# A fused top-k attention and MLP kernel: the second weights converted later, two conversion operations and a check moved in GpSimd's queue, and 16 more units turned by VectorE

## The chip, the cores and the metric

The kernel runs on one core of a Trainium2 chip. The metric is the device time of one execution in microseconds, the median of several runs. One further execution was profiled, and all views below are of it. The engines are named TensorE (PE in the profile, PEld for its weight loads), VectorE (DVE), ScalarE (ACT), GpSimd (POOL) and SyncE (SP, which only issues DMAs here).

## The reference, cut to what matters

```python
scores = scale * np.matmul(q, k.transpose(0, 1, 3, 2))      # q, k, v: (8, 8, 576, 64), float32
kth = np.partition(scores, -32, axis=-1)[..., -32:-31]
scores = np.where(scores >= kth, scores, -1e9)
attn = np.exp(scores - scores.max(-1, keepdims=True))
attn = attn / (attn.sum(-1, keepdims=True) + 1e-9)
x = np.matmul(attn, v)                                       # bridged to (8, 576, 512)
xn = (x - x.mean(-1, keepdims=True)) / np.sqrt(x.var(-1, keepdims=True) + 1e-6) * g_ln
out = x + np.maximum(xn @ w_ch1, 0) @ w_ch2                  # 512 -> 2048 -> 512
```

The MLP's two weights arrive as 64-bit floats and are turned into float32 on the chip.

## The kernel before

**Units and steps.** The attention is cut into 160 units. A unit is 128 query rows of two heads (two tiles of 128 x 576 scores), or, for the last 64 rows of a sequence ("rest"), the 64 rows of both heads in one tile. Four units of one kind, one for each pair of heads, or longer groups such as rows [0-1, rest] and [2-3], follow each other batch by batch. The main loop runs over steps n; in step n several units stand at different stages, and each engine executes its instructions in the order in which the loop writes them.

- `scores` (L395, copied by L376) is done two steps ahead: TensorE makes the score halves, ScalarE copies them from PSUM to `sc`.
- `halve` (L416, L417) at the end of step n makes the larger and the smaller half of the next unit's scores. `select` in four parts (L438, L424, L430) then finds the 32nd largest score by maxima of eight and replacements. All of this is on VectorE. The pool of `hi` has two buffers.
- `prepare` (L450, L451) scales the threshold and the maximum on ScalarE, `mask` is a Relu on ScalarE (L486) and a subtraction on GpSimd (L489), and `weigh` is the exponential with its row sum (L497). The pool of `e` has two buffers.
- A unit's weights must then be turned for the product with v. Either TensorE does it (`turn`: L555 for the main part, copied by L567; L584 for the ends, copied by L585), or the unit is "moved": VectorE transposes 32 x 32 blocks (`move`, L528), SP sends them to DRAM and three steps later `bring` fetches them in turned order, and TensorE turns the ends only. Units from the 40th on are moved, but for rest units and the last unit of a group: 72.
- `values` (L609, L616) is the product with v for a group; `take_values` (L624) copies it, `place` turns it back (L651) and scales it into the rows x (L628). A group's `lag` is the number of steps from its last unit to `values`: 2 for units 0-7, then 3, or 4 where the next job's first unit is moved.

**The note.** `watch` (L457, GpSimd) notes for each unit whether the eighth maximum of the smaller half could have mattered. Every 16 units `settle_watch` (L466) reduces the notes; at the end `tell` decides whether a slower second pass runs (it doesn't for these inputs). Before, step n begins with the note of unit n-1:

```python
        if mk and doubt is not None:
            watch(mk)
```

**Weights.** 32 pieces of 128 x 512, 16 of w1, then 16 of w2. `fetch` is a DMA of 512 KB; `split` runs three activations (L163 size, L164 low word, L167 sign), for w1 a fourth that multiplies the sign by the norm's gain (L169), then a clamp on GpSimd (L170); `shift` is on VectorE (L173); `join` is an integer addition and a multiplication on GpSimd (L179, L181). The list `batches` says which pieces are split in which step: four ahead of the loop, one or two in steps 0-7, two in each of steps 8-15. A batch's pieces are joined one step later. Up to step 6 the joins stand at a step's end.

**MLP blocks.** When a block of 256 finished rows is there, its matmuls go into the list `todo`, and `fill` puts some of them between the attention's instructions, as many as `slot` plans from estimated costs. The first block is given at step 9 (`gives_first`); its path values, take_values, place, statistics (L679), turning (L713), hidden matmuls (L754) is straight-line there, and its rows of w2 are needed for its second product (L793). After it GpSimd forms sums of w2's quarters (`form_pair`, L965-L968, four operations a pair, four pairs), which later blocks use in a product with seven instead of eight parts (L911, with sums L841-L847 on GpSimd). After the last unit only MLP work is left.

Of the kernel before, what the change touches and what calls it, by code (L numbers as in the profile page):

```python
# [10 lines left out]
ALU = mybir.AluOpType  # L11
# [8 lines left out]
STEEP = 2.0**90  # L20
# [9 lines left out]
def compute(  # L30
# [12 lines left out]
    nc = tc.nc  # L43
    P = nc.NUM_PARTITIONS
# [46 lines left out]
    def const(shape, name):  # L91
        return consts.tile(shape, FP32, tag=name, name=name)
# [5 lines left out]
    def turned():  # L98
        return brief("tp")
# [5 lines left out]
    ends = const([P, P], "ends")  # L105
    nc.gpsimd.memset(ends[:], 0.0)
    if doubt is not None:
        watched = const([P, 34], "watched")
        nc.gpsimd.memset(watched[:], -1.0)
    ident = const([P, P], "ident")  # L110
    make_identity(nc, ident[:])
# [10 lines left out]
    class Piece:  # L122
# [26 lines left out]
        def split(self):  # L149
            i = self.i  # L150
            high = self.raw[:, :, 1].bitcast(FP32)
            if i < NF:
                self.size = hpool.tile([P, DM], U32, tag="h", name="size")[:]
                self.low = wt_rows[:, i % 8]
                homes = ((opool, "o"), (opool, "o"), (rpool, "r"), (rpool, "r"), (xtpool, "xT"))
            else:
                self.size = wt_rows[:, 2 * i % 8].bitcast(U32)
                self.low = wt_rows[:, (2 * i + 1) % 8]
                homes = ((opool, "o"), (opool, "o"), (rpool, "r"))
            pl, tag = homes[i % len(homes)]  # L160
            self.sign = pl.tile([P, DM], FP32, tag=tag, name="sign")
            size_f = self.size.bitcast(FP32)
            nc.scalar.activation(size_f, high, AF.Abs)  # L163
            nc.scalar.activation(  # L164
                self.low, self.raw[:, :, 0], AF.Copy, bias=2.0, scale=2.0**-51
            )
            nc.scalar.activation(self.sign[:], high, AF.Sign)  # L167
            if self.i < NF:
                nc.scalar.mul(self.sign[:], self.sign[:], gcol[:, self.c : self.c + 1])  # L169
            nc.gpsimd.tensor_scalar(size_f, size_f, HIGH_MAX, HIGH_MIN, ALU.min, ALU.max)  # L170

        def shift(self):
            nc.vector.tensor_scalar(  # L173
# [22 lines left out]

    batches = {}
    queue = list(pieces)
    for n in range(-1, NF):
        count = 4 if n < 0 else 1 + (n + 1) % 2 if n < NF // 2 else 2  # L200
        batches[n], queue = queue[:count], queue[count:]
    assert not queue

# [2 lines left out]
    def weights(n, phase):  # L206

        now, before = batches.get(n, []), batches.get(n - 1, [])  # L210
        if phase == 0:
            for x in batches.get(n + 1, []):
                x.fetch()
            for x in now[0::2]:
                x.split()
        elif phase == 1:
            for x in before:
                x.join()
            for x in now[1::2]:
                x.split()  # L220
# [149 lines left out]
    def scores(u):  # L370

        u.sc = scpool.tile([P, 2, S], FP32, tag="sc", name="sc")
        made = [score_half(u, s) for s in range(2)]
        for t in range(len(u.tiles)):
            for s in range(2):
                nc.scalar.copy(  # L376
                    u.sc[:, t, s * HALF : (s + 1) * HALF], made[s][t][:, 0:HALF]
                )
# [67 lines left out]
    def prepare(u):  # L446

        nt = len(u.tiles)
        u.bias, u.edge = u.top[:, 0:nt, 0], u.thr[:, 0:nt, 7]
        nc.scalar.mul(u.edge, u.edge, STEEP)  # L450
        nc.scalar.mul(u.bias, u.bias, -scale)  # L451

    def watch(u):

        nt = len(u.tiles)
        c = 1 + 2 * (u.i % 16)
        nc.gpsimd.tensor_tensor(  # L457
            watched[:, c : c + nt], u.hi[:, 0:nt, HALF + 7], u.thr[:, 0:nt, 7], ALU.subtract
        )
        if u.i % 16 == 15 or u.i == N - 1:  # L460
            u.ends_watch = True

    def settle_watch():

        for out, first, op in ((0, 0, ALU.max), (33, 1, ALU.min)):
            nc.vector.tensor_reduce(  # L466
                watched[:, out : out + 1], watched[:, first : first + 33],
                mybir.AxisListType.X, op,
            )

    def tell():

        w = hpool.tile([P, J * P], FP32, tag="h", name="tell")
        nc.gpsimd.memset(w[:], 0.0)
        nc.vector.tensor_scalar(w[:, 1:2], watched[:, 33:34], -1.0e38, None, ALU.is_le)
        nc.vector.tensor_scalar(w[:, 0:1], watched[:, 0:1], 0.0, None, ALU.is_ge)
        nc.vector.tensor_tensor(w[:, 0:1], w[:, 0:1], w[:, 1:2], ALU.max)
        ps = brief("tell")
        nc.tensor.transpose(ps[:, 0:P], w[:, 0:P], ident[:])
        nc.vector.tensor_reduce(w[0:1, P : P + 1], ps[0:1, 0:P], mybir.AxisListType.X, ALU.max)  # L480
        nc.vector.tensor_copy(doubt, w[0:1, P : P + 1])
# [64 lines left out]
    def turn(u):  # L546

        g = u.group
        i0 = place_of(u)
        q0 = i0 * 32  # L550

        def part(t):
            ps = turned()
            for c in range(J):
                nc.tensor.transpose(  # L555
                    ps[:, c * P : (c + 1) * P], u.e[:, t, c * P + t * R : (c + 1) * P + t * R],
                    ident[:],
                )
            if u.rest:
                both = ps[:].rearrange("p (c h n) -> p h c n", h=2, n=R)  # L560
                for h in range(2):
                    nc.scalar.copy(
                        g.blocks[:, h, i0 : i0 + R // 32],
                        both[:, h].rearrange("p c (i n) -> p i c n", n=32),
                    )
            else:
                nc.scalar.copy(  # L567
                    g.blocks[:, t, i0 : i0 + P // 32],
                    ps[:].rearrange("p (c i n) -> p i c n", c=J, n=32),
                )  # L570

        def last():
            ps = turned()
            if u.rest:
                nc.tensor.transpose(ps[0:R, 0:P], u.e[:, 0, JP:S], ident[:])
                nc.tensor.transpose(ps[:, P : 2 * P], u.e[:, 0, JP - R : S], ident[:])
                for h in range(2):
                    nc.scalar.copy(
                        g.pt[h * R : (h + 1) * R, 2 * J, q0 : q0 + R],
                        ps[h * R : (h + 1) * R, h * (P + R) : h * (P + R) + R],  # L580
                    )
            else:
                ends = u.e[:].rearrange("p t n -> p (t n)")[:, JP : JP + P]
                nc.tensor.transpose(ps[:, 0:P], ends, ident[:])  # L584
                nc.scalar.copy(g.pt[:, 2 * J, q0 : q0 + P], ps[:, 0:P])  # L585

        heads = () if u.moved else range(len(u.tiles))
        return [lambda t=t: part(t) for t in heads] + [last]

    xs, xps, rs, oTr, dr = {}, {}, {}, {}, {}  # L590

# [30 lines left out]
    def take_values(g):  # L622
        g.oT = otpool.tile([P, GQ], FP32, tag="oT", name="oT")
        nc.scalar.copy(g.oT[:, 0 : g.nq], g.av[:, 0 : g.nq])  # L624
# [405 lines left out]
    CONVERTING = max(n for n in batches if batches[n]) + 2  # L1030
    EARLY = jobs[NHP].first

    for u in units[jobs[5 * NHP].first :]:
        u.moved = not u.rest and u is not u.group.units[-1]


# [44 lines left out]
    def at(i):  # L1081
        return units[i] if 0 <= i < N else None
# [10 lines left out]
    def due(n):  # L1093

        return units[n + 2 : n + 3]
# [87 lines left out]
    for n in range(END):  # L1185
# [15 lines left out]

        moved = ex is not None and ex.moved

        if n:
            for x in due(n):
                scores(x)
        if g:
            values(g)
        if n in brings:
            brings.pop(n)()  # L1210
            turn(at(n - 3))[-1]()
        if quick:
            take_values(g)
        if u:
            select(u, 0)
        if quick:
# [8 lines left out]
        if n in keeps:  # L1225
            keep_heads(keeps[n])
        if doubt is not None and at(n - 2) and at(n - 2).ends_watch:
            settle_watch()
            if n == N + 1:
                tell()  # L1230
        if mk and doubt is not None:
            watch(mk)
        if early:
            prepare(ex)
            for t in range(2):
                mask(ex, t)
            if n < gives_first - 1:
                weights(n, 0)
            for t in range(2):
                weigh(ex, t)  # L1240
        if not early or n == gives_first - 1:
            weights(n, 0)
        fill()
        if mk and not early:
# [4 lines left out]
            mask(mk, 1)  # L1249
        if g and not quick:  # L1250
            take_values(g)
        if parts:
            parts[0]()
        if ex and ex.rest:
# [25 lines left out]
        fill()  # L1280
        if n in ends_due:
            fill_ends(ends_due.pop(n))
        if g and not quick:
            place(g)
        if late:
            place_rest(late.job.b, late.job.hp)
        fill(1 if g or late else 0)
        if mk and mk.i >= EARLY:
            weigh(mk, 0)
        fill()  # L1290
        if len(parts) > 2:
            parts[1]()
# [20 lines left out]
        fill()  # L1313
        if u:
            select(u, 3)
        if nxt:
            halve(nxt)
        if n < LAZY:
# [76 lines left out]
```

## Time and profile before

| what | value |
| --- | --- |
| median of 3 runs | 1632.91 us (1632.14 to 1634.82) |
| the profiled execution's own time | 1631.76 us |
| span of the profiled execution | 1629.8 us |
| busy in it: PE, DVE, ACT, POOL | 1499.9, 1348.7, 1108.6, 1029.1 us |
| mean granted TensorE clock | 0.97 |
| DMA traffic | 211.49 MB in the span |

Steps are told apart by VectorE's halving: the halving of unit n+1 is the last thing of step n on VectorE. It starts at 20.1 us for step 0, 101.0 for step 7, 111.0 for step 8, 133.8 for step 9, 143.6, 160.3, 173.3, 185.9, 200.0 and 212.6 for steps 10 to 15, 221.9, 230.6, 235.1 and 244.9 for steps 16 to 19, 315.3 for step 26, 467.2 for step 45 and 1468.2 for step 158. A chain line gives start, duration and what ran; a wait line gives who waited for whom, the total, how often, and the longest.

### The profile page before, as it was taken

How to read it: one execution, taken by the hardware profiler on the slowest of the kernel's cores; microseconds unless marked ns; L12 is line 12 of the kernel's file. 1: busy time of each engine (PE TensorE's matmuls, PEld its weight loads, DVE VectorE, ACT ScalarE, POOL GpSimd, SP SyncE). 2: the span in 40 equal slices, each digit the busy share in tenths (PEclk: the TensorE clock that was granted, in tenths of full speed). 3: DMA queues.
4: the chain of work that ended last, by engine and by line, in shares of the span. 5: the costliest groups of instructions: out<-in, count | busy, mean ns of one | idle time of the engine just before them, and what ended most of it. 6: DMA issues, size and time to landing. Idle time of an engine off the chain costs nothing.

```text
span 1629.8 us, 27190 instructions
## 1 busy us (share of the span) xinstructions
PE 1499.9 (92%) x7898; PEld 1131.1 (69%) x7898; DVE 1348.7 (83%) x3939; ACT 1108.6 (68%) x3032; POOL 1029.1 (63%) x1473
## 2 busy tenths in 40 slices
PE   2556889899999999999999999999999999999997
PEld 1334646577767677777777777777777777778886
DVE  6866679698999999999999998998899999992000
ACT  6885767678777676777666867677667776764311
POOL 4775875865666676767765747465657666656344
PEclk9867899999999999999999999999999999999999
DMA  8432335312365456545564465546554455432211
GB/s 216 134 99 82 111 80 118 118 57 68 85 167 180 120 148 166 162 145 142 152 189 133 137 152 172 163 116 175 146 171 149 127 155 159 155 98 85 66 39 54
DMA packets 355685, 211.49 MB, mean 130 GB/s; under 512 B 247492, under 2 KB 327880, under 8 KB 355528
## 3 DMA queue, kind: packets, MB, share of 16 engines
q1 hardware_dynamic: 350792, 209.08, 45.2%
q8 instruction: 65, 1.06, 0.3%
q10 hardware_dynamic: 4736, 0.59, 0.2%
q14 instruction: 92, 0.75, 0.2%
HBM read 145.62 MB, written 63.96 MB: 129 GB/s over the span
## 4 chain that ended last, share of the span: by engine, by line
PE 64%; POOL 15%; ACT 12%; DVE 7%; issue 1%; DMA 1%; ACTq 0%; SPq 0%; POOLq 0%; DVEq 0%
PE hps L754 23%; PE ops L911 19%; PE scps L395 8%; POOL e L489 6%; PE av L609 5%; ACT e L486 3%; PE tp L555 3%; DVE m L438 2%; DVE hi L424 2%; PE av L616 2%; ACT sc L376 2%; POOL h L847 1%; ACT e L497 1%; POOL w L181 1%; PE xo L651 1%
## 5 line engine op out<-in xcount | busy, mean ns | idle before, releaser
L489 POOL TENSOR_TENSOR e<-e,sc 128x576 f32<-128x576 f32 x288 | 423.1, 1486 | 441.1 <-ACT e L486 434.0
L754 PE MATMUL hps<-xT,w 128*128 128x256 f32 x2304 | 546.2, 384 | 7.3 <-ACT xT L716 7.3
L754 PEld LDWEIGHTS hps<-xT,w 128*128 128x128 f32 x2304 | 425.0, 192 | 74.1 <-issue 11.5
L438 DVE MAX8 m<-hi 128x8 f32<-128x296 f32 (+1 forms) x1152 | 471.2, 444 | 0.2
L424 DVE MATCH_REPLACE8 hi<-m,hi 128x288 f32<-128x288 f32 (+1 forms) x864 | 377.7, 442 | 0.0
L911 PE MATMUL ops<-w,h 128*128 128x256 f32 x1360 | 322.3, 383 | 1.4 <-POOL h L847 1.4
L911 PEld LDWEIGHTS ops<-w,h 128*128 128x128 f32 x1360 | 251.3, 192 | 40.1 <-issue 5.8
L376 ACT COPY sc<-scps 128x288 f32<-128x288 f32 x576 | 199.1, 407 | 99.3 <-PE scps L395 77.7
L497 ACT ACTIVATE e<-e,m 128x576 f32<-128x576 f32 x288 | 224.8, 781 | 59.5 <-POOL e L489 58.0
L486 ACT ACTIVATE e<-sc,m 128x576 f32<-128x576 f32 x288 | 212.4, 769 | 0.0
L416 DVE TENSOR_TENSOR hi<-sc 128x576 f32<-128x576 f32 (+1 forms) x160 | 135.4, 846 | 59.7 <-POOL watched L457 55.3
L609 PE MATMUL av<-pt,vb 128*64 128x256 f32 (+2 forms) x1088 | 147.2, 412 | 5.9 <-ACT pt L567 4.8
L417 DVE TENSOR_TENSOR lo<-sc 128x576 f32<-128x576 f32 (+1 forms) x160 | 144.1, 901 | 0.0
L555 PE MATMUL tp<-ident,e 128*128 128x128 f32 x576 | 94.0, 291 | 47.0 <-ACT e L497 47.0
L395 PE MATMUL scps<-kT,late_qT 64*128 64x288 f32 (+3 forms) x832 | 129.2, 419 | 8.6 <-ACT pt L567 6.0
L777 ACT ACTIVATE h<-hps 128x512 f32<-128x512 f32 x144 | 85.2, 592 | 66.7 <-PE hps L754 65.7
L911 PE MATMUL ops<-wt,s 128*128 128x256 f32 x544 | 129.3, 381 | 0.0
L555 PEld LDWEIGHTS tp<-ident,e 128*128 128x128 f32 x576 | 76.8, 150 | 69.7 <-ACT e L497 52.3
L528 DVE STREAM_TRANSPOSE sc<-e 128x512 f32<-128x512 f32 x144 | 94.3, 687 | 33.4 <-POOL h L847 16.7
L609 PEld LDWEIGHTS av<-pt,vb 128*64 128x64 f32 x1088 | 72.8, 141 | 67.2 <-issue 15.5
L430 DVE MAX8 hi<-lo 128x8 f32<-128x288 f32 x288 | 117.7, 444 | 0.0
L395 PEld LDWEIGHTS scps<-kT,late_qT 64*128 64x128 f32 (+1 forms) x832 | 72.3, 171 | 61.8 <-issue 18.7
(104 smaller groups left out, 1887.4 us busy)
## 6 DMA issues: line engine op xcount, KB each, us to landing
turned<-sc SPq DMA_DIRECT2D x72, 512.0 KB, 2.9
pt<-turned SPq DMA_DIRECT2D x288, 128.0 KB, 2.7
w<-forms SPq DMA_DIRECT2D x136, 256.0 KB, 3.9
vb<-in_v_dram SPq DMA_DIRECT2D x68, 288.0 KB, 3.9
raw<-in_moe_w_ch_dram SPq DMA_DIRECT2D x32, 512.0 KB, 3.5
kT<-kept SPq DMA_DIRECT2D x36, 288.0 KB, 3.5
kin<-in_k_dram SPq DMA_DIRECT2D x128, 72.0 KB, 2.8
kept<-kT SPq DMA_DIRECT2D x32, 288.0 KB, 3.0
```

The source lines that it names most:

```text
L376: nc.scalar.copy(u.sc[:, t, s * HALF : (s + 1) * HALF], made[s][t][:, 0:HALF])
L395: nc.tensor.matmul(ps[i * R : i * R + ql, o : o + width], qT[r, q0 : q0 + ql], kT[r, k0 : k0 + width], start=True, stop=True,)
L417: nc.vector.tensor_tensor(lo, a, b, ALU.min)
L424: nc.vector.match_replace(x, m[:, t, :], x, LOWEST)
L438: nc.vector.max(m[:, t, :], u.hi[:, t, 0:width])
L486: nc.scalar.activation(u.e[:, t], u.sc[:, t], AF.Relu, bias=u.edge[:, t : t + 1], scale=-STEEP)
L489: nc.gpsimd.tensor_tensor(u.e[:, t], u.e[:, t], u.sc[:, t], ALU.subtract)
L497: nc.scalar.activation(u.e[:, t], u.e[:, t], AF.Exp, bias=u.bias[:, t : t + 1], scale=-scale, accum_out=g.den[:, col : col + 1],)
L555: nc.tensor.transpose(ps[:, c * P : (c + 1) * P], u.e[:, t, c * P + t * R : (c + 1) * P + t * R], ident[:],)
L609: nc.tensor.matmul(av[h * D : (h + 1) * D, 0 : g.nq], vb[:, h * (J + 1) + c, :], g.blocks[:, h, 0 : g.nq // 32, c, :], start=(c == 0), sto ...
L754: nc.tensor.matmul(ps[0][:, side * N : (side + 1) * N], w1[:, c, f * P : (f + 1) * P], self.xT[:, c, 0:N], start=(c == 0), stop=(c == NC - 1),
L911: nc.tensor.matmul(bank[name][:, 0:Q], a(j), rhs, start=first and j == 0, stop=(j == G - 1), skip_group_check=not first,)
```

## The change

- `batches`: steps 8 and 9 convert nothing, the sixteen pieces of w2 are converted in steps 10 to 17.
- `split`: the multiplication by the gain goes from ScalarE to GpSimd, and the clamp is written right behind the first activation.
- The note of unit n is written at the end of step n, behind its last selection. Its tile has two halves that take turns. The scaled threshold goes to column 6 of the tile, no longer over the threshold in column 7.
- Units from the 8th on are moved (88 in place of 72), so the lag of the groups of that stretch is 4.
- Up to step 9 `values` stands ahead of `scores`. The ends of a moved unit are turned at the old place, but copied behind the masks and `take_values` (`turn_ends` returns the copy).
- `place` stands behind the first `weigh` and a `fill` rather than ahead of them. The weights' splits in step 8 follow the common order, which is without effect as that batch is empty.

```diff
+            nc.gpsimd.tensor_scalar(size_f, size_f, HIGH_MAX, HIGH_MIN, ALU.min, ALU.max)
...
             if self.i < NF:
-                nc.scalar.mul(self.sign[:], self.sign[:], gcol[:, self.c : self.c + 1])
-            nc.gpsimd.tensor_scalar(size_f, size_f, HIGH_MAX, HIGH_MIN, ALU.min, ALU.max)
+                nc.gpsimd.tensor_scalar(
+                    self.sign[:], self.sign[:], gcol[:, self.c : self.c + 1], 1.0,
+                    ALU.mult, ALU.mult,
+                )
...
-    for n in range(-1, NF):
-        count = 4 if n < 0 else 1 + (n + 1) % 2 if n < NF // 2 else 2
+    for n in range(-1, NF + 2):
+        count = 4 if n < 0 else 1 + (n + 1) % 2 if n < NF // 2 else 0 if n < NF // 2 + 2 else 2
...
-        u.bias, u.edge = u.top[:, 0:nt, 0], u.thr[:, 0:nt, 7]
-        nc.scalar.mul(u.edge, u.edge, STEEP)
+        u.bias, u.edge = u.top[:, 0:nt, 0], u.thr[:, 0:nt, 6]
+        nc.scalar.mul(u.edge, u.thr[:, 0:nt, 7], STEEP)
...
-    for u in units[jobs[5 * NHP].first :]:
+    for u in units[EARLY:]:
         u.moved = not u.rest and u is not u.group.units[-1]
...
-        if n:
-            for x in due(n):
-                scores(x)
-        if g:
+        late_ends = None
+        ahead = due(n) if n else []
+        if g and n <= gives_first:
+            values(g)
+        if quick:
+            take_values(g)
+        for x in ahead:
+            scores(x)
+        if g and n > gives_first:
             values(g)
         if n in brings:
             brings.pop(n)()
-            turn(at(n - 3))[-1]()
-        if quick:
-            take_values(g)
+            late_ends = turn_ends(at(n - 3))
...
-        if mk and doubt is not None:
-            watch(mk)
...
         if g and not quick:
             take_values(g)
+        if late_ends:
+            late_ends()
...
+        fill(1 if g or late else 0)
+        if mk and mk.i >= EARLY:
+            weigh(mk, 0)
         if g and not quick:
             place(g)
         if late:
             place_rest(late.job.b, late.job.hp)
-        fill(1 if g or late else 0)
-        if mk and mk.i >= EARLY:
-            weigh(mk, 0)
...
         if u:
             select(u, 3)
+            if doubt is not None:
+                watch(u)
```

More of the change, by code (lines that the diff above doesn't have):

```diff
@@ L107, in compute @@
     if doubt is not None:
-        watched = const([P, 34], "watched")
+        watched = const([P, 2, 34], "watched")
         nc.gpsimd.memset(watched[:], -1.0)
@@ L455, in watch @@
         nt = len(u.tiles)
-        c = 1 + 2 * (u.i % 16)
+        half, c = u.i // 16 % 2, 1 + 2 * (u.i % 16)
         nc.gpsimd.tensor_tensor(
-            watched[:, c : c + nt], u.hi[:, 0:nt, HALF + 7], u.thr[:, 0:nt, 7], ALU.subtract
+            watched[:, half, c : c + nt], u.hi[:, 0:nt, HALF + 7], u.thr[:, 0:nt, 7], ALU.subtract
         )
@@ L461, in watch, with settle_watch @@
             u.ends_watch = True
-    def settle_watch():
+            u.half = half
+    def settle_watch(half):
         for out, first, op in ((0, 0, ALU.max), (33, 1, ALU.min)):
             nc.vector.tensor_reduce(
-                watched[:, out : out + 1], watched[:, first : first + 33],
+                watched[:, half, out : out + 1], watched[:, half, first : first + 33],
                 mybir.AxisListType.X, op,
@@ L474, in tell @@
         nc.gpsimd.memset(w[:], 0.0)
-        nc.vector.tensor_scalar(w[:, 1:2], watched[:, 33:34], -1.0e38, None, ALU.is_le)
-        nc.vector.tensor_scalar(w[:, 0:1], watched[:, 0:1], 0.0, None, ALU.is_ge)
-        nc.vector.tensor_tensor(w[:, 0:1], w[:, 0:1], w[:, 1:2], ALU.max)
+        nc.vector.tensor_scalar(w[:, 2:4], watched[:, :, 33], -1.0e38, None, ALU.is_le)
+        nc.vector.tensor_scalar(w[:, 4:6], watched[:, :, 0], 0.0, None, ALU.is_ge)
+        nc.vector.tensor_reduce(w[:, 0:1], w[:, 2:6], mybir.AxisListType.X, ALU.max)
         ps = brief("tell")
@@ L572, in last, with turn_ends, copy @@
         def last():
-            ps = turned()
+            turn_ends(u)()
+        heads = () if u.moved else range(len(u.tiles))
+        return [lambda t=t: part(t) for t in heads] + [last]
+    def turn_ends(u):
+        q0 = place_of(u) * 32
+        g = u.group
+        ps = turned()
+        if u.rest:
+            nc.tensor.transpose(ps[0:R, 0:P], u.e[:, 0, JP:S], ident[:])
+            nc.tensor.transpose(ps[:, P : 2 * P], u.e[:, 0, JP - R : S], ident[:])
+        else:
+            ends_e = u.e[:].rearrange("p t n -> p (t n)")[:, JP : JP + P]
+            nc.tensor.transpose(ps[:, 0:P], ends_e, ident[:])
+        def copy():
             if u.rest:
-                nc.tensor.transpose(ps[0:R, 0:P], u.e[:, 0, JP:S], ident[:])
-                nc.tensor.transpose(ps[:, P : 2 * P], u.e[:, 0, JP - R : S], ident[:])
                 for h in range(2):
@@ L582, in last @@
             else:
-                ends = u.e[:].rearrange("p t n -> p (t n)")[:, JP : JP + P]
-                nc.tensor.transpose(ps[:, 0:P], ends, ident[:])
                 nc.scalar.copy(g.pt[:, 2 * J, q0 : q0 + P], ps[:, 0:P])
-        heads = () if u.moved else range(len(u.tiles))
-        return [lambda t=t: part(t) for t in heads] + [last]
+        return copy
     xs, xps, rs, oTr, dr = {}, {}, {}, {}, {}
@@ L1227, in compute @@
         if doubt is not None and at(n - 2) and at(n - 2).ends_watch:
-            settle_watch()
+            settle_watch(at(n - 2).half)
             if n == N + 1:
                 tell()
-        if mk and doubt is not None:
-            watch(mk)
         if early:
@@ L1236, in compute @@
                 mask(ex, t)
-            if n < gives_first - 1:
-                weights(n, 0)
+            weights(n, 0)
             for t in range(2):
                 weigh(ex, t)
-        if not early or n == gives_first - 1:
+        if not early:
             weights(n, 0)
```

## The prediction

> **What bounds it now.** I read the busy shares by slice first, then the same by stage, then the waits, then the chain. The bound is never one engine for the whole run.
>
> ```profile
> PE   2556889899999999999999999999999999999997
> ...
> DVE  6866679698999999999999998998899999992000
> ...
> PEclk9867899999999999999999999999999999999999
> ```
>
> TensorE is full from the eighth slice on; its idle time (1629.8 - 1499.9 = 130 us) lies mostly in the first 300 us, where its granted clock is low as well. VectorE is full in the middle and empty in the tail.
>
> ```profile
> 20.10:101.00 80.90, 37.22 (x167) 23.25 (x165) 64.25 (x194) 69.48 (x163) 61.40 (x63) 0.83 0.53 145
> 101.00:133.80 32.80, 18.23 (x68) 9.79 (x66) 19.55 (x60) 23.79 (x58) 20.09 (x20) 0.69 0.32 103
> 133.80:244.90 111.10, 90.81 (x403) 59.71 (x404) 77.87 (x227) 77.91 (x199) 80.04 (x84) 0.86 0.31 91
> 244.90:315.30 70.40, 63.40 (x356) 41.51 (x355) 56.21 (x178) 45.60 (x131) 51.09 (x66) 0.95 0.42 103
> 315.30:467.20 151.90, 148.01 (x838) 112.01 (x836) 137.99 (x427) 122.46 (x349) 94.06 (x143) 0.99 0.35 93
> 467.20:1468.20 1001.00, 982.08 (x5306) 748.80 (x5305) 970.20 (x2793) 715.12 (x2012) 645.27 (x950) 1.00 0.53 151
> 1468.20:1629.80 161.60, 151.87 (x744) 130.72 (x743) 12.21 (x40) 43.22 (x101) 74.34 (x137) 0.99 0.20 61
> ```
>
> The stages are cut at the halving (L416): steps 1-7, 8-9, 10-19, 20-26, 27-45, 46-158, the rest. The columns are length, PE, weight loads, DVE, ACT, POOL, clock, DMA share, GB/s. Before 244.9 us no engine is full: each waits for another, ScalarE closest to full (86% in steps 1-7). After 467 us VectorE (97%) and TensorE (98%) are both full. By instruction order, the MLP matmuls issued up to step 45 are equal in both kernels, and the order after that differs only in where copies, placing and the note stand. So the change is worth what it takes from the first 467 us, plus a little per step later.
>
> ```profile
> ACT pt L585 <- PE tp L584: 76.2, 50, 4.5
> ...
> DVE hi L416 <- POOL watched L457: 55.3, 27, 7.1
> ACT m L450 <- POOL watched L457: 54.8, 35, 5.1
> ...
> PE xo L651 <- ACT oT L624: 18.8, 26, 3.7
> ```
>
> From the chain between 20 and 134 us:
>
> ```profile
> 103.82 0.72 ACT sign L169
> ...
> 116.20 0.56 ACT wt L163
> ...
> 121.89 3.61 PE av L609 x16
> ...
> 128.41 0.55 ACT wt L163
> ```
>
> The conversion's activations stand on the chain itself, ahead of the masks and of the first block's values.
>
> **Factor on GpSimd (steps 0-8).** Sixteen multiplications by the gain (L169, 722 ns) leave ScalarE; sixteen come to GpSimd. On the chain between 20.1 and 101 us they stand six times in full and once in part, 6 x 0.72 + 0.57 = 4.9 us; three of the first four pieces add 2.2 us before that. The nearest rows for the new cost are tensor_scalar on GpSimd, 698 ns (L170) and 712 ns (L688, with a pointer operand): 16 x 0.70 = 11.2 us, against 80.9 - 61.4 = 19.5 us of idle GpSimd in steps 1-7. Queued behind each are a joining pair and the next mask's subtraction. Nothing taken back gives -7.1, all of it on the path +4; I take -5.5, nearer the first, since ScalarE (86%) is busier than GpSimd (76%).
>
> The added work can also block VectorE. Two-input operations on VectorE show it: the minimum (L417) has a median of 751 ns and a longest of 1982 ns, the latter kind beside GpSimd work (1.81 us at 134.65). The Trainium skill (SBUF — State Buffer, Terms) says that the port pair shared by VectorE and GpSimd is locked for a whole instruction and the loser blocks fully. By that rule the sum would lose up to 16 x 0.70 = 11 us, by the row's mean excess (954 - 751 = 0.2 us per operation) about 3 us; as VectorE idles 16.7 us in steps 1-7, I add nothing.
>
> **The pause (steps 8-9).** Batches 8 and 9 are empty, and w2's sixteen pieces move to steps 10-17. From the chain leave: the two splits at 116.2 and 118.4 (3.4 us), the one at 128.4 (1.7), and 0.7 for a factor; values ahead of scores takes away the 1.3 us of scores before 121.89. The sum is -7.1; bounds 0 (another wait ends there) and -11.7 (the hidden matmuls start at 139.3 behind a stalled sign, and could start near 127.6). I take -6.5.
>
> **The pause given back (steps 10-19).** The eight conversion steps remain. Steps 12-15 take 13.0, 12.6, 14.0 and 12.6 us, 13.1 on average; the ones behind them that convert nothing 9.3 and 8.6. Now I count 9.5 for step 10, six steps (11-16) of 12.6, two (17, 18, with half-size rest units) of 9.5 and 7 for step 19: 111.1, as before. The 0.5 us off a step is two copies (L567, 584 ns each) fewer on every second step. Bounds: 13.8 and 12.0 per step, +7 and -4; I take 0.
>
> **Sixteen more moved units (8 to 39).** Each adds to VectorE two block transposes (L528, 687 ns), 1.37 us: 22.0 us in all, 5.5 in steps 10-17, 16.5 from step 20 on. Each removes eight PE transposes, 0.88 us by the chain at full clock (four in 0.44) up to 1.98 at half clock: 14 to 32 us; and two ScalarE copies, 1.17 us. I put the TensorE time into no stage: before step 20 TensorE waits for the others, behind it VectorE sets the pace. It adds five DMAs on SP (512 KB out, four of 128 KB back, 2.9 and 2.7 us to landing), 80 in all and about 16 MB, at a DMA share of 0.31 to 0.42. The send stands on SP behind VectorE's transposes, so the fetches of raw weights and of K wait behind it; values come a step later (lag 4), which covers the two landings. If that cover fails, up to 5.6 us per group are exposed.
>
> Work taken from TensorE while it is not full may cost clock: the rows grant 0.69 in steps 8-9 and 0.86 in steps 10-19. The Trainium skill (TensorE: Matmul & The Clock Gate, Part 1) says the throttled state is the default and activity releases it. By that rule steps 10-19 could fall to the 0.69 of the row above, 90.8 x (0.86/0.69 - 1) = 22 us more TensorE time; by the rows, more hidden matmuls stand in steps 9-14 than before, so I charge none.
>
> **The note (watch) re-timed.** Before, it stands in the next step, so VectorE's halving and ScalarE's prepare wait for it behind GpSimd's forms and joins. Now it stands at the end of its own step, and the scaled edge goes to another column, so prepare need not wait. In steps 20-26 VectorE idles 14.2 us, all of it for the note; in steps 27-45 13.9, for the note too. In 20-26 the 14.2 can go and 4.1 (three moves) come: -10 at most, 0 if the mask's subtraction or the forms (four of 1.27 us a pair) hold it; I take -6. In 27-45: -13.9 + 9 x 1.37 = -1.6; bounds +4 and -6, I take -2. GpSimd now waits for the last maximum with forms and joins queued behind it; before, it waited 11.6 us so in the whole run, so I charge nothing more.
>
> **Later copies and placing.** Delaying the copy of the ends does not remove ScalarE's 76.2 us: the next mask writes the same buffer, and now waits for that PE turn itself. Placing behind the first weighing and one filling item covers PE's 18.8 us for oT, 11.6 of them in steps 46-158. VectorE is full there, so I take -3, bounds -8 and +3. The second half of the note's tile and the other reductions touch single columns: nothing.
>
> **Sum.** -5.5 - 6.5 + 0 - 6 - 2 - 3 = -23.0 on the profiled execution's own 1631.76 us gives 1608.8. That execution is 1.15 us below the median of 1632.91, so I forecast 1610.
>
> **Rivals.**
> *VectorE becomes the bound* (slower). It takes on 22.0 us, and its idle time between 133.8 and 467.2 us, 33.2 + 14.2 + 13.9 = 61.3, stays, as each wait for the note becomes one for a mask or a weighing. For it: VectorE waits 16.1 us in ten places for L497 before moves now. Against it: the notes' waits are real and the note moves. Price +22 - 12 at the front = +10, 1643. It decides if that idle falls by less than 10 us.
> *Front only.* Steps 0-9 gain 12 us, the moves use up what the note frees: 1621. For it: steps 27-45 forecast almost nothing already.
> *Decoupled conversion.* In steps 10-19 all four engines hold 78 to 91 us of work in 111. If the pause, fewer copies and the note let them overlap up to 93, the sum gains 18 more: 1592. Against it: joins hold GpSimd 5.1 us a step in both.
> *Nothing visible*: the front's gain and the moves' cost cancel, 1633. That the turning does not move is excluded by the order: 176 block transposes, 144 before.
>
> **Chances.** Forecast (1600 to 1615) 0.44, front only 0.20, decoupled 0.12, VectorE bound 0.20, nothing 0.04. A measurement here can tell about 0.2% (3.3 us) from no change. Faster 0.76, same 0.04, slower 0.20. The range reaches from the decoupled case, 1592, to most of the VectorE case, 1640, the lighter part of either left out.
>
> **What would show it.** L169's successor on GpSimd near 0.7 us and no ScalarE chain through it; step 9 at 16 us rather than 22.7; the halving's wait for the note under 10 us; steps 11-16 near 12.6; VectorE idle between steps 10 and 45 near 31 us; the stretch from step 46 to 158 within 1% of 1001 us. I am wrong if conversion steps exceed 14 us, or the moves wait for weighing.

## The result, and the profile after

The changed kernel takes 1618.61 us (median of 4 runs, 1617.56 to 1622.38), the kernel before 1633.55 us beside it; the ratio is 0.9913, with a 95% interval of 0.9894 to 0.9932. The forecast was 1610, with a range of 1592 to 1640. The sign and the range held, but little of the gain lies where the forecast put it.

The page of the changed kernel, the same three rows by slice as before (each slice 40.4 us):

```profile
PE   3548978899989899999999999999999999999997
...
DVE  7877879999999999999999999999999999982000
...
PEclk9768989899989999999999999999999999999999
```

VectorE is now full from the seventh slice on. TensorE still has its idle time at the start: 1615.8 - 1486.2 = 129.6 us of it, against 130 before.

The same stages (steps 1-7, 8-9, 10-19, 20-26, 27-45, 46-158, the rest), cut at the changed kernel's own halvings, with the columns length, PE, weight loads, DVE, ACT, POOL, clock, DMA share, GB/s:

```profile
19.90:104.30 84.40, 40.40 (x168) 25.16 (x166) 70.04 (x194) 58.26 (x143) 76.24 (x74) 0.78 0.49 132
104.30:134.60 30.30, 15.79 (x65) 10.08 (x66) 19.80 (x58) 19.88 (x54) 19.38 (x18) 0.68 0.25 83
134.60:242.10 107.50, 92.23 (x410) 56.72 (x409) 85.22 (x238) 80.69 (x207) 83.44 (x86) 0.90 0.49 147
242.10:311.40 69.30, 57.62 (x302) 40.65 (x302) 68.58 (x182) 42.32 (x123) 57.41 (x69) 0.89 0.56 151
311.40:466.10 154.70, 142.03 (x751) 104.27 (x751) 152.50 (x446) 109.12 (x322) 96.11 (x138) 0.94 0.52 152
466.10:1454.10 988.00, 978.04 (x5311) 751.22 (x5311) 978.35 (x2793) 711.59 (x2016) 672.02 (x951) 1.00 0.53 153
1454.10:1615.80 161.70, 151.87 (x744) 130.72 (x743) 12.50 (x40) 43.13 (x101) 74.34 (x137) 0.98 0.20 61
```

Against before, in order: +3.5, -2.5, -3.6, -1.1, +2.8, -13.0 and 0 us. Step 45 ends at 466.1 us instead of 467.2: the first 45 steps, in which the forecast expected 20 us, gave 1. The other 13 come in steps 46 to 158, where both kernels do the same work. In steps 20-45 VectorE is busy for 221.1 of 224.0 us.

The waits of the changed kernel that answer to those shown of before:

```profile
ACT e L490 <- PE tp L592: 47.8, 31, 2.6
POOL watched L460 <- DVE m L441: 31.7, 27, 3.3
...
DVE hi L419 <- POOL watched L460: 8.3, 7, 3.6
PE xo L667 <- ACT oT L640: 7.8, 10, 3.2
```

The halving's wait for the note fell from 55.3 to 8.3 us, prepare's (54.8 us) is gone, TensorE's wait for the copied product (oT) fell from 18.8 to 7.8 us. New is GpSimd's own wait for the last maximum, 31.7 us where it was 11.6. ScalarE's 76.2 us for the turned ends became a wait of the next mask for the same turning (47.8 us).

So VectorE lost most of its idle time and still does not run ahead. Where that time went is in its busy time. The minimum of the halving, one two-input operation per unit, by the same stages (first the kernel before, L417, then the changed one, L420; busy time and count):

```profile
20.10:101.00 80.90, 5.25 (x7) 0.83 0.53 145
...
244.90:315.30 70.40, 5.25 (x7) 0.95 0.42 103
315.30:467.20 151.90, 12.77 (x19) 0.99 0.35 93
```

```profile
19.90:104.30 84.40, 7.79 (x7) 0.78 0.49 132
...
242.10:311.40 69.30, 12.12 (x7) 0.89 0.56 151
311.40:466.10 154.70, 17.61 (x19) 0.94 0.52 152
```

In steps 20-26 the same seven operations take 12.12 us instead of 5.25. The timeline of the changed kernel shows what stands beside one of them:

```profile
281.71 0.90 DVE L419 TENSOR_TENSOR hi<-sc 128x576 f32<-128x576 f32 x1
281.96 1.78 POOL L984 TENSOR_TENSOR form<-w,wt 128x512 f32<-128x512 f32 x1
282.54 1.82 DVE L420 TENSOR_TENSOR lo<-sc 128x576 f32<-128x576 f32 x1
283.70 1.91 POOL L493 TENSOR_TENSOR e<-e,sc 128x576 f32<-128x576 f32 x1
```

The minimum takes 1.82 us between two operations of GpSimd, which take 1.78 and 1.91 us; in the kernel before the same two lines take 1.27 and 1.49 us on average (spans on GpSimd are rough). In these steps of the kernel before, VectorE waited for the note, that is, until GpSimd was through with its forms, and then did both halves undisturbed. The whole of both traces agrees: none of the 256 halving operations of full size in either kernel takes over 0.79 us unless GpSimd works beside it for at least 0.75 us, and those of the kernel before with nothing on GpSimd beside them, 59 maxima and 31 minima, take 0.73 to 0.76 us.

### The profile page after: what moved, and what is told of

The parts are those of the page before. It is cut to its first block, busy times and chain, and to the rows that moved or that the text cites. A ratio compares the mean times of both kernels' runs of the same rounds, so it can differ in the third digit from the quotient of the medians.

```text
span 1615.8 us, 27078 instructions
## 1 busy us (share of the span) xinstructions
PE 1486.2 (92%) x7770; PEld 1124.1 (70%) x7770; DVE 1397.4 (86%) x3971; ACT 1076.2 (67%) x2984; POOL 1084.7 (67%) x1489
## 4 chain that ended last, share of the span: by engine, by line
PE 73%; POOL 10%; DVE 7%; ACT 6%; DMA 2%; issue 1%; SPq 0%; POOLq 0%; ACTq 0%; DVEq 0%
PE hps L770 27%; PE ops L927 22%; PE scps L398 9%; PE av L625 7%; POOL e L493 3%; PE tp L559 3%; PE av L632 2%; DVE m L441 2%; DVE hi L427 2%; POOL w L184 2%; ACT sc L379 1%; ACT e L490 1%; PE tp L729 1%; ACT e L501 1%; POOL wt L182 1%
## 5 line engine op out<-in xcount | busy, mean ns | idle before, releaser
L770 PEld LDWEIGHTS hps<-xT,w 128*128 128x128 f32 x2304 | 429.7, 193 | 69.5 <-issue 11.8
L490 ACT ACTIVATE e<-sc,m 128x576 f32<-128x576 f32 x288 | 212.3, 770 | 47.8 <-PE tp L592 47.8
L420 DVE TENSOR_TENSOR lo<-sc 128x576 f32<-128x576 f32 (+1 forms) x160 | 167.6, 1048 | 0.0
L419 DVE TENSOR_TENSOR hi<-sc 128x576 f32<-128x576 f32 (+1 forms) x160 | 142.9, 893 | 12.2 <-POOL watched L460 8.3
L532 DVE STREAM_TRANSPOSE sc<-e 128x512 f32<-128x512 f32 x176 | 114.3, 686 | 25.6 <-ACT e L501 25.6
L398 PE MATMUL scps<-kT,late_qT 64*128 64x288 f32 (+3 forms) x832 | 124.8, 413 | 7.5 <-ACT x L644 4.2
L559 PE MATMUL tp<-ident,e 128*128 128x128 f32 x448 | 75.7, 297 | 53.3 <-ACT e L501 53.3
L398 PEld LDWEIGHTS scps<-kT,late_qT 64*128 64x128 f32 (+1 forms) x832 | 70.4, 169 | 61.5 <-issue 23.8
L398 PE MATMUL scps<-kT,qT 64*128 64x288 f32 x512 | 92.8, 460 | 21.0 <-DVE qT L328 11.6
```

Source lines behind the costliest of these rows:

```text
L398: nc.tensor.matmul(ps[i * R : i * R + ql, o : o + width], qT[r, q0 : q0 + ql], kT[r, k0 : k0 + width], start=True, stop=True,)
L419: nc.vector.tensor_tensor(hi, a, b, ALU.max)
L420: nc.vector.tensor_tensor(lo, a, b, ALU.min)
L490: nc.scalar.activation(u.e[:, t], u.sc[:, t], AF.Relu, bias=u.edge[:, t : t + 1], scale=-STEEP)
L770: nc.tensor.matmul(ps[0][:, side * N : (side + 1) * N], w1[:, c, f * P : (f + 1) * P], self.xT[:, c, 0:N], start=(c == 0), stop=(c == NC - 1),
```

## The experiments

Each ran beside the kernel before on the same chip; over the three rounds the kernel before took 1632.4 to 1632.7 us. Times are medians of four runs, stages are read from one profile each. Four executions of the changed kernel lie 4.8 us apart, and the profiles of kernels that have the same order from step 46 on take 988.0 to 991.0 us in steps 46 to 158. So a difference of 3 us in the total, or in those steps, shows nothing alone.

**The factor back on ScalarE.**

```diff
-                nc.gpsimd.tensor_scalar(
-                    self.sign[:], self.sign[:], gcol[:, self.c : self.c + 1], 1.0,
-                    ALU.mult, ALU.mult,
-                )
+                nc.scalar.mul(self.sign[:], self.sign[:], gcol[:, self.c : self.c + 1])
```

> The changed kernel with the multiplication by the gain back on ScalarE; all else as changed. Theory A (GpSimd, idle 8.1 us of 84.4 in steps 1-7 of the changed kernel, became the bound there): step 7 ends about 3 us earlier than the 104.3 us of the changed kernel, GpSimd idle there rises to about 17 us, and the time falls by 0 to 4 us from 1618.6, depending on how much of it the later steps pass on. Theory B (as forecast, ScalarE's chain is the worse place): step 7 ends 5 us later, and the time rises by 5 us.

1621.08 us, ratio 0.9924 (0.9905 to 0.9944). Neither theory held: step 7 ends at 104.3 us with the factor on either engine, though GpSimd idles 18.1 us instead of 8.1. In this order something other than the factor's place sets these steps.

**w2's pieces in steps 8 to 15 again.**

```diff
-    for n in range(-1, NF + 2):
-        count = 4 if n < 0 else 1 + (n + 1) % 2 if n < NF // 2 else 0 if n < NF // 2 + 2 else 2
+    for n in range(-1, NF):
+        count = 4 if n < 0 else 1 + (n + 1) % 2 if n < NF // 2 else 2
```

> The changed kernel with w2's pieces split in steps 8 to 15 again; all else as changed. Theory A (the pause is what gained 6 us between steps 8 and 19): step 9 is longer by about 5 us, the end of step 19 is 3 to 6 us later than 242.1 us, and the time rises by 0 to 6 us. Theory B (the pause only shifts the conversion): the end of step 19 and the time stay within 2 us.

1623.02 us, ratio 0.9942 (0.9924 to 0.9959). By step 19 it is theory A: that step ends at 245.3 us, 3.2 later. Its place was wrong, though: step 9 took 1.0 us longer, not 5, and step 11 ended 11.9 us later than with the pause, of which 8.7 came back by step 19. At the end of step 45 only 0.6 us is left (466.7 us against 466.1). Steps 46 to 158 take 2.9 us more, which kernels alike there show without it, so the time doesn't confirm the pause's worth.

**The note at the start of the next step again**, its edge column left as changed.

```diff
             select(u, 3)
-            if doubt is not None:
-                watch(u)
...
+        if mk and doubt is not None:
+            watch(mk)
         if early:
```

> The changed kernel with the note of unit n-1 at the start of step n again (the two halves of its tile and the edge's own column stay). Theory A (the note's place is what gains in steps 96 to 158): VectorE waits some 50 us in all for the note in its halving again, steps 96-128 take about 299 us rather than 292.9, and the time rises by 8 to 14 us. Theory B (the later copies and placing gain there): the wait returns but the time rises by less than 4 us.

1618.63 us, ratio 0.9909 (0.9892 to 0.9925): no difference. The halving's wait for the note came back to only 18.5 us, steps 96-128 took 292.9 us as in the changed kernel. Where the note stands does not carry the gain here.

**72 moved units again.**

```diff
-    for u in units[EARLY:]:
+    for u in units[jobs[5 * NHP].first :]:
```

> The changed kernel with 72 moved units rather than 88. Theory A (VectorE sets the pace of steps 20 to 45, and the sixteen units cost it there what the note frees): step 45 ends 8 to 16 us earlier than 466.1 us, and the time falls by 5 to 15 us from 1618.6. Theory B (TensorE's total work sets the time, 14 to 32 us of it come back): the time rises by 10 to 20 us.

1624.05 us, ratio 0.9943 (0.9926 to 0.996). Both theories fell: the sixteen moves are worth some 5 us, not the 10 to 20 of TensorE's work, and not a loss. Steps 20-26 did shorten to 60.5 us, but steps 27-45 lengthened to 160.6: without the moves the two halving operations took 46.0 us there rather than 31.2. Step 45 ends 2.1 us later than in the changed kernel; the rest comes after it, where up to 3 us can be chance.

**Placing ahead of the weighing again.**

```diff
-        fill(1 if g or late else 0)
-        if mk and mk.i >= EARLY:
-            weigh(mk, 0)
         if g and not quick:
             place(g)
         if late:
             place_rest(late.job.b, late.job.hp)
+        fill(1 if g or late else 0)
+        if mk and mk.i >= EARLY:
+            weigh(mk, 0)
```

> The changed kernel with place and place_rest again ahead of the filling item and the first weighing. Theory A (later placing is what gained 13 us in steps 96 to 158): steps 96-158 take about 575 us rather than 563, TensorE waits for the copied product (oT) some 10 us again in steps 46-158, and the time rises by 8 to 13 us from 1618.6. Theory B (the ends' later copy gained it): the time rises by less than 3 us.

1624.0 us, ratio 0.9946 (0.9929 to 0.9962). TensorE waits 16.5 us for oT again; steps 96-158 take 568.5 us rather than 562.8. Its undoing gives back 5.7 of the 12.8 us gained there, between the two theories.

**The ends copied ahead of the masks again.**

```diff
-            late_ends = turn_ends(at(n - 3))
+            turn_ends(at(n - 3))()
```

> The changed kernel with the ends of a moved unit copied right behind their turning again, ahead of the masks. Theory A (later placing gained steps 96 to 158): ScalarE waits for the turned ends some 60 us again, the masks waited as long anyway for the same turning, and the time rises by less than 3 us. Theory B (the later copy gained): the time rises by 8 to 13 us and steps 96-158 take about 575 us.

1619.67 us, ratio 0.9922 (0.9905 to 0.9939): no difference that can be measured, as theory A said. ScalarE waits 82.5 us for the turned ends again.

**Scores ahead of values up to step 9 again.**

```diff
-        if g and n <= gives_first:
-            values(g)
-        if quick:
-            take_values(g)
         for x in ahead:
             scores(x)
-        if g and n > gives_first:
+        if g:
             values(g)
...
+        if quick:
+            take_values(g)
```

> The changed kernel with scores ahead of values up to step 9 again. In the changed kernel step 7 ends 3.3 us later than before, with the factor on either engine. Theory A (values ahead of scores delays the score copies that ScalarE starts a step with, in steps 3 to 8): step 7 ends at about 101 us, step 9 grows by 1 to 3 us, and the time changes by less than 3 us. Theory B (something else, GpSimd beside VectorE's halving, slows steps 1 to 7): step 7 still ends at about 104 us.

1614.12 us, ratio 0.9894 (0.9878 to 0.9911), all four runs under the changed kernel's fastest. Step 7 ends at 103.1 us rather than 104.3, and steps 8-9 take 25.9 us rather than 30.3: against both theories, the first block's path is shorter with the scores first. The two intervals overlap; the stages are clearer. Step 9 ends at 129.0 us here and at 128.5 in the last kernel below, which has this order too, but at 134.6 to 136.7 in the changed kernel and the seven others with values first. The waits of steps 1-7, first of the changed kernel, then of this one:

```profile
ACT sc L379 <- PE scps L398: 11.1, 9, 3.1
```

```profile
ACT sc L379 <- PE scps L398: 3.8, 6, 0.7
```

TensorE's matmuls run in the order in which the loop writes them. With values in front, the scores come behind them, and ScalarE, which begins its step with the copies of the scores, waits 7.3 us longer. Of the 4.4 us in steps 8-9, 3.6 lie ahead of step 9's values: the turning in front of them ends 17.7 us after the start of step 8 with values first, and 14.1 us with the scores first. Behind it the orders differ by only 0.8 us, although the scores then stand in the way. From the chain, first of the changed kernel, then of this one:

```profile
121.98 3.99 PE av L625 x16
...
126.60 1.22 PE scps L398 x8
```

```profile
117.18 2.22 PE scps L398 x8
119.40 2.25 PE av L625 x16
```

The sixteen matmuls of values take 3.99 us at a granted clock of 0.53 where they stand first, and 2.25 us at 0.84 behind the scores.

**Less work on GpSimd in the forming of w2's sums.**

```diff
-        tt(t1, b12, b11, ALU.subtract)
-        tt(t2, b22, t1, ALU.subtract)
-        tt(t3, t2, b11, ALU.subtract)
-        tt(t4, b21, t2, ALU.subtract)
+        nc.gpsimd.memset(t1, 0.0)
+        nc.gpsimd.memset(t2, 0.0)
+        nc.gpsimd.memset(x[:], 0.0)
```

> The changed kernel in which the four subtractions of each pair of forms are left out and three memsets stand in their place on GpSimd (the sums of w2's quarters are not formed). Theory A (VectorE's two halving operations are slowed by GpSimd work beside them; in steps 20-26 they take 19.6 us, 10.5 before): with 2 to 3 us less GpSimd work in each of four steps, they fall to 11 to 15 us there and the stage of 69.3 us shortens by 3 to 8 us. Theory B (their duration has another cause): they stay at 18 to 20 us.

One execution, 1609.79 us; the kernel leaves the sums out. The minimum by stage, as above, for steps 20-26:

```profile
242.30:306.00 63.70, 7.53 (x7) 1.00 0.63 172
```

The seven operations take 7.53 us instead of 12.12, both halving operations together 14.7 instead of 19.6, and the stage 63.7 us instead of 69.3. Theory A: what stands on GpSimd beside them stretches them. The edit changes both how long GpSimd works and what it does (memsets for two-input operations), and no run here separates the two; the one minimum with memsets beside it for nearly its whole length takes 0.74 us.

**Later placing alone, on the kernel before.**

```diff
+        fill(1 if g or late else 0)
+        if mk and mk.i >= EARLY:
+            weigh(mk, 0)
         if g and not quick:
             place(g)
         if late:
             place_rest(late.job.b, late.job.hp)
-        fill(1 if g or late else 0)
-        if mk and mk.i >= EARLY:
-            weigh(mk, 0)
```

> The kernel before with the later placing alone (the clamp's line and the note's second half also stand in it, which change no waiting). Theory A (later placing alone carries the gain of steps 96 to 158): these take about 563 us rather than 575.6 and the time is 1620 to 1624, 9 to 13 us under before. Theory B (placing carries about half, as its undoing gave back 5.8 of 12.8 us there, and the note the rest): 568 to 571 us there, time 1626 to 1629.

1624.93 us, ratio 0.9948 (0.9931 to 0.9965). The time lies between the theories; steps 96-158 take 566.4 us, nearer theory B.

**The re-timed note alone, on the kernel before.**

```diff
-        nc.scalar.mul(u.edge, u.edge, STEEP)
+        u.bias, u.edge = u.top[:, 0:nt, 0], u.thr[:, 0:nt, 6]
+        nc.scalar.mul(u.edge, u.thr[:, 0:nt, 7], STEEP)
...
-        if mk and doubt is not None:
-            watch(mk)
...
             select(u, 3)
+            if doubt is not None:
+                watch(u)
```

> The kernel before with the re-timed note alone (end of its own step, two halves, the edge in its own column). Theory A (placing alone carries the late gain): VectorE's wait for the note falls from 55 us to under 15, its two halving operations lengthen in return, and the time stays within 3 us of before. Theory B (the note carries the rest): steps 96-158 take 567 to 571 us and the time is 1625 to 1629. As forecast on record: steps 20-26 shorten by up to 10 us, since no move is added here.

1622.9 us, ratio 0.9934 (0.9917 to 0.995), 9.8 us under before: theory B, and 2 us beyond its range; steps 96-158 take 566.5 us. The stages show the trade (20-26 and 27-45, columns as above):

```profile
242.80:305.50 62.70, 58.38 (x326) 39.39 (x324) 62.70 (x178) 44.39 (x129) 50.05 (x63) 0.95 0.47 116
305.50:463.20 157.70, 150.88 (x844) 113.74 (x841) 155.98 (x427) 122.86 (x349) 105.27 (x147) 0.98 0.34 89
```

Steps 20-26 fall from 70.4 to 62.7 us. Steps 27-45 rise from 151.9 to 157.8: VectorE's idle time falls from 13.9 to 1.7 us, and its two halving operations rise from 26.7 to 45.1.

**Both.**

> The kernel before with the later placing and the re-timed note. Theory A (placing alone): as with placing alone, within 2 us. Theory B (each carries its part): about the sum of the two, 1619 to 1623, with steps 96-158 at about 563 us.

1617.0 us, ratio 0.9899 (0.9882 to 0.9915), 15.7 us under before; 7.8 and 9.8 make 17.6. Theory B, though steps 96-158 take 565.2 us: there the parts don't add, as placing alone takes 9.2 us off them, the note alone 9.1 and both 10.4. These two parts give as much as the whole change does.

**Scores first and the factor on ScalarE**, all else as changed.

> The changed kernel with scores ahead of values up to step 9, and the factor back on ScalarE. With scores first GpSimd idles only 3.4 us of 82.2 in steps 1-7. Theory A (there the factor makes GpSimd the bound): these steps take 80 to 81 us, 1 to 2 us less than with scores first alone, and the time is 1612 to 1614. Theory B (as forecast on record, ScalarE's chain is worse): they take 86 to 88 us and the time is 1618 to 1620.

1613.72 us, ratio 0.9877 (0.9861 to 0.9894). With the scores out of the way the factor's place can be seen in steps 1-7 (first with the factor on GpSimd, then on ScalarE):

```profile
20.90:103.10 82.20, 38.20 (x168) 22.92 (x166) 68.12 (x194) 61.28 (x151) 78.75 (x76) 0.77 0.54 146
```

```profile
21.10:100.50 79.40, 37.12 (x167) 23.22 (x165) 69.14 (x193) 69.03 (x163) 66.34 (x63) 0.79 0.54 144
```

GpSimd is busy for 78.75 of 82.2 us in the first, 66.34 of 79.4 in the second, which is 2.8 us shorter; steps 8-9 give 2.1 of it back, and the times (1614.12 and 1613.72) can't be told apart. In steps 1-7 this is theory A.

## Why the prediction was right, and where it was not

The sum was -23, the result about -15, and that it came so near is in good part luck: the terms up to step 45, -20 together, measured -1, and the stretch behind them, -3, measured -13. 1618.6 us lies outside the forecast case's own 1600 to 1615 and next to the price of the rival *front only* (1621), but that mechanism did not come either: step 9 ends 0.8 us later than before, not 12 earlier. By its own terms:

- **Factor, -5.5: measured +3.3 at the end of step 7.** Two steps failed. "I take -5.5, nearer the first, since ScalarE (86%) is busier than GpSimd (76%)" priced the added operation rightly at 0.70 us, but left out blocking ("I add nothing"). The new operation and the joining multiplication (first before, L181, then changed, L184), with the shortest, median and longest in ns:

```profile
L170 POOL TENSOR_SCALAR sign<-sign,gcol x16: 692/698/1662, 14.6 to 109.4; 128x512 f32<-128x512 f32 x16
```

```profile
L181 POOL TENSOR_TENSOR w<-size,sign x16: 1262/1270/1335, 25.6 to 118.8; 128x512 f32<-128x512 f32 x16
```

```profile
L184 POOL TENSOR_TENSOR w<-size,sign x16: 1267/1304/2911, 24.7 to 121.0; 128x512 f32<-128x512 f32 x16
```

Nine of the sixteen new operations take 692 to 698 ns; the other seven, each beside VectorE's shift of a piece (L176), take 927 to 1662. The means are 874 ns, and 1624 for the multiplication (1274 before). GpSimd's busy time in steps 1-7 grew by 14.8 us, from 61.4 to 76.2. And the order of values and scores, credited with -1.3 us in the next term alone, acts in steps 3 to 9. With scores first, the factor's place costs 2.8 us in steps 1-7 rather than gaining 5.5.

- **Pause, -6.5 and 0: measured -2.5 and -3.6**, together near the forecast, but not by the forecast's path: undone, it gives back 0.9 us in steps 8-9 and 1.6 in steps 10-19. What failed is that values ahead of scores would shorten the path. With scores first and the factor on ScalarE, as before, steps 8-9 take 28.0 us, 4.8 less than before, close to the 5.1 us of the splits that left the chain.
- **Moved units.** Forecast as 22.0 us more on VectorE (measured: 22.0, 32 operations of 686 ns) paid out of the freed waits, with TensorE's relief put nowhere (measured: with the moves TensorE is busy 1486.2 us, without them 1499.7). Undone they cost 5.4 us, so the whole was a gain. The lower clock that was weighed for steps 10-19 did not come (0.90, before 0.86), but in steps 20-26 and 27-45 the granted clock is 0.89 and 0.94, where it was 0.95 and 0.99, and with the moves undone it is 0.96 and 0.98. The rival "VectorE becomes the bound" was right on what bounds steps 20-45 (idle 0.7 and 2.2 us) and wrong on its test: the idle time between steps 10 and 45 fell by 36 us, from 61.3 to 25.2 (forecast near 31).
- **Note, -6 and -2 in steps 20-26 and 27-45: measured -1.1 and +2.8.** The step that failed is "as VectorE idles 16.7 us in steps 1-7, I add nothing": blocking was left out of these stages as well. VectorE's busy time in steps 10-45 rose by 34.2 us: the moves are 22.0 of it, and the durations of the two halving operations grew by 14.8 (54.5 to 69.3 us; neighbours overlap a little, so these make more than the whole). Much of the freed wait was spent beside GpSimd.
- **Later copies and placing, -3: measured -13 after step 45, mis-sized and misplaced.** The reason given against more, that VectorE is full there, did not hold: in steps 96-128 it idled 25.9 us before, most of it in these two waits:

```profile
DVE hi L416 <- POOL watched L457: 13.7, 10, 4.9
DVE sc L528 <- ACT e L497: 9.7, 8, 2.6
```

Placing alone leaves 4.9 us of the first and none of the second, the note alone leaves 2.0 and none, both together none. And the note was given nothing after step 45. On the kernel before, placing alone gives 7.8 us and the note alone 9.8. The copy of the ends gives nothing, as its wait only moved, which was the argument made.

- **The signs it named.** The halving's wait (8.3 us, under 10) and the new operation's median came as said. Step 9 took 18.8 us rather than 16, steps 11-16 between 8.2 and 14.5 us (one over the 14 us set as a sign of being wrong), and steps 46-158 shrank by 1.3%, more than the 1% allowed.

The rule that the prediction weighed and set aside fits better than what it chose. The Trainium skill (SBUF — State Buffer, Terms) says that the pair of ports that VectorE and GpSimd share is locked for a whole instruction, and that the loser blocks fully. The runs agree in size: beside GpSimd the minimum takes 1.82 us rather than 0.75 in the place shown, 1.07 us more, and it shrinks when GpSimd's forms are left out. They don't show the ports themselves. The row's mean excess, 0.2 us, which the prediction preferred, is a mean over the whole run; in steps 1-9 and 20-26 of that kernel each minimum took 0.75 us, so the row held nothing of what the change would bring there.

Two things stay open. Of the note's two edits, the place and the column, only the undoing of the place was run, and changed nothing; that points to prepare's removed wait, but the column was not run alone. And why the halving meets GpSimd more in some stages than in others (steps 129-158 lost 8.6 us of it) was not tested; how the two queues stand to each other is the likely reason, and no run here steers it.

## What to carry to other kernels

A wait between two engines may be what keeps them off a shared resource: before counting a removed wait as gain, ask what the freed engine will run beside. A mean duration holds only for the neighbours it was measured with. And putting one stage's work first on an in-order engine puts its waits first too: here the scores first, although they looked like 1.3 us in front of the longer path, made steps 8-9 shorter by 4.4 us.

## What was not expected of the hardware

Not every VectorE operation is stretched. With two-input GpSimd operations beside them for nearly their whole length, the maxima (MAX8), the replacements and the block transposes of the changed kernel keep their durations: 444, 444 and 686 ns on average, and 445, 443 and 687 with none beside them. The two-input halving takes 0.75 us alone and up to 1.97, and the shift of a piece (L176), which has one input, 0.41 to 0.43 us alone and up to 1.49. What sets the two kinds apart no run here shows. The time shows as a longer operation, not as idle time, and GpSimd's operations lengthen too (e<-e,sc takes 1.91 us in the place shown, 1.48 on average).
